# Attention and Mish MLP on one core: stores issued by ScalarE, loads a pair further ahead, an earlier DMA turn of q and k

## The chip, the cores and the metric

The kernel runs on one core of a Trainium2 chip. A core has five engines that work beside each other: TensorE (PE in the profile; PEld is its weight load), VectorE (DVE), ScalarE (ACT), GpSimd (POOL) and SyncE (SP), which issues most DMAs. Each engine takes its instructions in order. The metric is the device time of one execution in microseconds (us); a lower time is better. Three runs of the kernel before gave 464.16, 464.88 and 459.46 us, a median of 464.16.

## The reference

Inputs are q, k and v of 8 batches x 12 heads x 448 positions x 64, and the weights w_in (768 x 2048) and w_out (2048 x 768), all in float32. What is computed:

```python
scores = q @ k.T / sqrt(64)                   # per batch and head, 448 x 448
m = max(scores, axis=-1)
e = exp(scores - m)
attn = e / (sum(e) + exp(-m) + 1e-9)          # softmax with one more term in the sum
x = (attn @ v), heads side by side            # 3584 tokens x 768
h = x @ w_in                                  # 3584 x 2048
g = h * tanh(log(1 + exp(h)))                 # Mish
out = g @ w_out                               # 3584 x 768, float32
```

## The kernel before, in words

**Units.** Two heads side by side make a pair (128 partitions of q and k); six pairs make a batch, 48 pairs the whole. Three pairs are a unit (`UNIT_PAIRS`), so a batch has two units, and units 0 to 15 hold the attention; two more run out the MLP at the end. The loop variable is `u`, the unit's first pair is `p0`, and `nxt = p0 + 3` is the first pair of the next unit. Units u = 6 to 15 are the "joined" ones (`JOINED_FROM` is 6). The change concerns these.

**One joined unit** has two stretches.

- The *exponential stretch* follows the list `JOINED` (line 625), an order written out by hand. Its entries: `("s", n)` issues the products q k^T of step n (four steps per pair, twelve in all) on TensorE; `mA`, `mB`, `m` take row maxima on VectorE; `eA`, `eB`, `e` are the exponentials on ScalarE; `("fill", n)` puts n chunks of the second matmul (g @ w_out, line 543) of an older batch on TensorE; `("copy", i)` copies a finished w_out group from PSUM to the SBUF tile `o_sb` on VectorE (line 522) and, when a tile of 128 rows is complete, stores it (line 507); `("av", i)` is attn @ v of pair i of the unit before, `("avc", i)` its copy to xT; `("load", i)` loads a pair and casts one; `("turn", i)` turns q and k of a pair by DMA.
- The *Mish stretch* (from line 841) computes eight tiles of x @ w_in (line 442), each followed by Mish on ScalarE (line 481). Beside them VectorE and GpSimd normalise the unit's e, and SP issues the DMA transposes of e into eT (line 390), one per pair. Here the next unit's q and k are turned too: most pairs by TensorE (line 224) in front of the tiles f = 2, 4 and 6, with copies by VectorE and ScalarE; the pairs in `TURN_BY_DMA` (from pair 21 on the first of each unit, and pair 46) by a DMA transpose (line 237).

**Loads and casts.** `load_pair(p)` is three DMAs of 224 KB (q, k, v in float32), issued by SP, with four buffers per tensor. `cast_pair(p)` is three casts to bf16 on GpSimd (lines 201 to 207 and 188). q_bf and k_bf of the pair are what TensorE or the DMA turns; v_bf is wanted a unit later. In a joined unit the three `load` entries load the pairs p0 + 3, 4 and 5, which are the next unit's; the second and the third entry cast the pair loaded by the entry before, and the last pair, `nxt + 2`, is cast in the Mish stretch (line 875).

**Queues.** All loads, e's transposes, q's and k's DMA turns and the stores are issued by SP, in the order in which the program has them; a DMA that waits for its data holds up all behind it. Only the last tile's smaller parts are stored by ScalarE. A tile of 128 rows takes two store DMAs, as rows of one DMA share a segment of 112. Two such tiles are complete in most joined units, one in u = 6, 10 and 14.

**PSUM.** Eight banks of 128 x 512 float32. In the Mish stretch tile f goes into the banks `JOINED_MISH_BANK = (7, 0, 4, 2, 6, 1, 7, 6)`; bank 2 and bank 3 hold the scores of step 9, banks 0 and 1 those of step 8, banks 4 and 5 those of step 10.

Of the kernel before, what the change touches and what calls it, by code (L numbers as in the profile page):

```python
# [15 lines left out]
UNIT_PAIRS = 3  # L16
# [3 lines left out]
def kernel(  # L20
# [9 lines left out]
    nc = tc.nc  # L30
# [203 lines left out]
    def turn_by_dma(p):  # L234

        qk = qk_all[:, p % UNIT_PAIRS]
        nc.sync.dma_start_transpose(
            out=qk.rearrange("c s (t q) -> c (s t) q", q=SP_),
            in_=qk_bf[:, p % N_CAST].rearrange("q s t h d -> q (s t h d)"),
        )  # L240
        qkT[p] = qk[:, 0, :], qk[:, 1, :]
# [250 lines left out]
            out=mids[g][:, :, 64 * half : 64 * half + 64], in_=gT[b][:, :, at : at + 64]  # L492
        )

    def store_rows(g, i, o_sb, cols):

        parts, r = [], i * 128
        while r < (i + 1) * 128:
            n = min((i + 1) * 128, (r // SP_ + 1) * SP_) - r
            parts.append((r, n))  # L500
            r += n
        queues = [nc.sync, nc.scalar if (g, i) == (B // 2 - 1, 6) else nc.sync]
        for queue, (r, n) in zip(queues, sorted(parts, key=lambda part: -part[1])):
            seg = r // SP_
            b, t, c0 = 2 * g + seg // NT, seg % NT, r % SP_
            rows = out[b * S : (b + 1) * S, :].rearrange("(c t) m -> t c m", t=NT)
            queue.dma_start(
                out=rows[t, c0 : c0 + n, cols], in_=o_sb[r - i * 128 : r - i * 128 + n, cols]
            )
# [3 lines left out]
    def mm2_group(pieces, bank=None):  # L513

        st = {"at": 0, "o": bank, "evacs": []}

        def evac(g, i, q0, nq, at, last):
            cols, n_cols = slice(q0 * NQ, (q0 + nq) * NQ), nq * NQ
            if (g, i) not in o_sbs:
                o_sbs[g, i] = [o_pool.tile([128, d_model], FP32, tag="o_sb", name="o_sb"), 0]  # L520
            o_sb, have = o_sbs[g, i]
            nc.vector.tensor_copy(out=o_sb[:, cols], in_=st["o"][:, at : at + n_cols])  # L522
            if last and bank is None:
                mo_free.append(st["o"])
            o_sbs[g, i][1] = have + nq
            if (g, i) == (B // 2 - 1, 6):
                store_rows(g, i, o_sb, cols)
            elif have + nq == 24:
                store_rows(g, i, o_sb, slice(0, d_model))

        def chunk(k, f0, f1):
            g, i, q0, nq = pieces[k]
            if st["o"] is None:
                flush_late()
                st["o"] = mo_take()
            if i < 3:
                src, c0 = gT[2 * g], i * 128
            elif i == 3:
                src, c0 = mids[g], 0
            else:  # L540
                src, c0 = gT[2 * g + 1], i * 128 - S
            for ff in range(f0, f1):
                nc.tensor.matmul(  # L543
                    st["o"][:, st["at"] : st["at"] + nq * NQ],
                    lhsT=src[:, ff, c0 : c0 + 128],
                    rhs=w_out_sb[:, ff, q0 * NQ : (q0 + nq) * NQ],
                    start=(ff == 0), stop=(ff == FF_T - 1),
                )
            if f1 == FF_T:
                last = k == len(pieces) - 1  # L550
                args = (g, i, q0, nq, st["at"], last)
                st["evacs"].append(lambda: evac(*args))
                st["at"] += nq * NQ
                if last and bank is None:
                    late.extend(st["evacs"])

        step = 2
        chunks = [
            (lambda k=k, f0=f0: chunk(k, f0, f0 + step), pieces[k][3] / 6)
            for k in range(len(pieces))  # L560
            for f0 in range(0, FF_T, step)
        ]
        return chunks, st["evacs"]
# [8 lines left out]
    for g in range(B // 2):  # L572
# [50 lines left out]
        [],  # L623
    )
    JOINED = (
        ("mA", 1), ("fill", 2), ("mA", 0), ("fill", 1), ("mB", 0), ("fill", 1), ("eA", 1),
        ("load", 0), ("mB", 1), ("fill", 2), ("eA", 0), ("mB", 2), ("fill", 1), ("eB", 1),
        ("mA", 2), ("fill", 2), ("eB", 0), ("fill", 1), ("copy", 0), ("fill", 3), ("eB", 2),
# [4 lines left out]
        ("fill", 1), ("mB", 6), ("fill", 1), ("eA", 4), ("fill", 1), ("copy", 1), ("s", 11),  # L633
        ("eB", 6), ("load", 2), ("fill", 1), ("m", 11), ("fill", 1), ("eB", 5), ("fill", 1),
# [4 lines left out]
    )  # L639
    PART_BANK = (7, 6, 2)  # L640
    AV_BANK = (7, 3, 6)
# [79 lines left out]
    for u in range(UNITS_PER_B, N_UNITS + 2 * UNITS_PER_B):  # L721
# [16 lines left out]
        for what, arg in JOINED if joined else ():  # L738
            at, idx = p0 + arg, p0 * STEPS + arg
            heads = {"A": (0,), "B": (1,)}.get(what[-1], (0, 1))  # L740
            if what == "s":
                held[arg] = score_products(idx)
            elif what[0] == "m":
                score_maxima(*held[arg], heads)
            elif what[0] == "e":
                exps(idx, heads)
            elif what == "fill":
                for _ in range(arg):
                    filler.popleft()[0]()
            elif what == "copy":  # L750
                for evac in copies[arg]:
                    evac()
            elif what == "av":
                held["av", arg] = av_pair(at - UNIT_PAIRS, bank=joined_banks[AV_BANK[arg]])
            elif what == "avc":
                held["av", arg]()
            elif what == "load":
                load_pair(at + LEAD - 1)
                if arg:
                    cast_pair(at + LEAD - 2)  # L760
            elif nxt + arg in TURN_BY_DMA:
                turn_by_dma(nxt + arg)
        if joined:
            expm_of(nxt - 1)

# [75 lines left out]
        for f in range(FF_U):  # L841
# [28 lines left out]
            if f in (1, 3, 5):  # L870
                if nxt + f // 2 not in TURN_BY_DMA:
                    transpose_pair(nxt + f // 2, bank=f // 2 % 2)
                    evac_qk(nxt + f // 2)
                if f == 1 and u >= first_mm2:
                    cast_pair(nxt + UNIT_PAIRS - 1)
            if not to_group and f in (4, 6):
                scores_ahead(nxt * STEPS + f // 2 - 1)
# [48 lines left out]
```

## Time and profile before

| What | Value |
|---|---|
| median of three runs | 464.16 us (459.46 to 464.88) |
| the profiled execution, its own time | 462.32 us |
| its span, first to last instruction | 460.5 us |
| mean granted TensorE clock | 0.989 |
| PE busy | 427.1 us (93%) |
| DVE, ACT busy | 340.7 and 342.3 us (74% each) |
| POOL busy | 185.7 us (40%) |
| DMA, mean over the span | 201 GB/s, 92.66 MB |
| stores by SP, by ScalarE | 57 and 3 |
| DMA transposes of e, of q and k | 43 and 10 |

The page's times come from one execution. "Busy" counts work only, not issuing a DMA: SP's DMA issues have durations of their own, in rows with SPq (ACTq for ScalarE's). In a row such as "PE b L224 <- POOL qk_bf L201" the left side waits, and the right side is what ended the wait; L224 is line 224 of the kernel. A wait in square brackets in a row of the order of time is the engine's idle time just before that row. Matmuls overlap in the rows: six products of 448 columns follow each other in 1.14 us, though one of them is shown with 0.35 us.

### The profile page before, as it was taken

The numbers are of one execution on the slowest core, as the hardware profiler recorded it, in microseconds if no ns is written. First come the engines' busy times: TensorE is split into PE (matmuls) and PEld (weight loads), VectorE is DVE, ScalarE is ACT, GpSimd is POOL, SyncE is SP. The second block draws the span as 40 slices with busy tenths as digits, with TensorE's granted clock in tenths as the row PEclk, the third lists the DMA queues.
The fourth block names the chain that finished last, engine by engine and source line by source line (L and its number), as shares of the span: only waits on it lengthen the run. The fifth ranks groups of instructions, "written<-read, shape, count | busy, mean of one in ns | idle before, by whom it ended". The sixth has DMA issues, their size and how long they took to land.

```text
span 460.5 us, 8732 instructions
## 1 busy us (share of the span) xinstructions
PE 427.1 (93%) x2968; PEld 234.4 (51%) x2968; DVE 340.7 (74%) x756; ACT 342.3 (74%) x908; POOL 185.7 (40%) x352
## 2 busy tenths in 40 slices
PE   4586798899999999899999999999999999999996
PEld 2243445444445555455555545564555455555565
DVE  4899968878797888668788888888888888421021
ACT  5998988988797788688888887897979878211300
POOL 3666839253517161534436271715454360000000
PEclk9997999999999999999999999999999999999999
DMA  8999999997999989998999999999999995950213
GB/s 210 220 202 221 282 188 248 200 212 174 223 263 217 246 171 227 266 207 234 185 270 211 219 227 206 247 219 254 229 265 201 244 206 135 177 133 0 70 36 103
DMA packets 211661, 92.66 MB, mean 201 GB/s; under 512 B 168352, under 2 KB 208160, under 8 KB 211616
## 3 DMA queue, kind: packets, MB, share of 16 engines
q1 hardware_dynamic: 204032, 85.76, 87.4%
q0 software_dynamic: 7488, 6.29, 9.3%
q8 instruction: 23, 0.38, 0.3%
q14 instruction: 22, 0.18, 0.1%
q10 hardware_dynamic: 96, 0.05, 0.0%
HBM read 45.61 MB, written 11.01 MB: 123 GB/s over the span
## 4 chain that ended last, share of the span: by engine, by line
PE 65%; DMA 10%; DVE 9%; ACT 6%; issue 3%; SPq 3%; POOL 2%; POOLq 0%; DVEq 0%
PE mo L543 24%; PE mo L442 17%; DMA q_f<-in_q_dram 7%; PE b L442 7%; DVE negm L335 6%; PE b L543 5%; ACT en L347 5%; PE b L304 4%; PE mo L423 2%; DMA k_f<-in_k_dram 2%; PE b L224 2%; PE b L423 2%; DMA eT<-en 1%; PE mo L312 1%; DVE xT L432 1%
## 5 line engine op out<-in xcount | busy, mean ns | idle before, releaser
L347 ACT ACTIVATE en<-b,negm 128x448 bf16<-128x448 f32 x216 | 133.9, 636 | 20.9 <-DVE negm L335 20.9
L335 DVE TENSOR_REDUCE negm<-b 128x1 f32<-128x448 f32 x216 | 120.6, 614 | 21.2 <-PE b L307 21.2
L543 PE MATMUL mo<-w_out_sb,gT 128*128 128x384 bf16 (+3 forms) x736 | 107.5, 298 | 2.4 <-DVE o_sb L522 1.8
L543 PEld LDWEIGHTS <-gT 128*128 128x128 bf16 x896 | 82.4, 98 | 51.8 <-issue 10.5
L442 PEld LDWEIGHTS <-w_in_sb 128*128 128x128 bf16 x768 | 72.6, 98 | 67.7 <-issue 7.3
L442 PE MATMUL mo<-xT,w_in_sb 128*128 128x448 bf16 x480 | 102.7, 357 | 0.8 <-DVE xT L432 0.3
L481 ACT ACTIVATE gT<-mo 128x448 bf16<-128x448 f32 x73 | 40.2, 551 | 54.1 <-PE mo L442 53.7
L384 POOL TENSOR_SCALAR en<-en,rden 128x448 bf16<-128x448 bf16 x109 | 67.3, 634 | 23.5 <-DVE rden L378 15.5
L386 DVE TENSOR_SCALAR en<-en,rden 128x448 bf16<-128x448 bf16 x227 | 71.5, 384 | 0.7
L442 PE MATMUL b<-xT,w_in_sb 128*128 128x448 bf16 x282 | 58.8, 353 | 0.2 <-DVE xT L432 0.2
L347 ACT ACTIVATE en<-sc,negm 128x448 bf16<-128x448 f32 x84 | 52.5, 642 | 4.0 <-DVE negm L335 2.6
L522 DVE COPY o_sb<-mo 128x384 f32<-128x384 f32 (+3 forms) x54 | 25.8, 492 | 40.0 <-PE mo L543 39.4
L335 DVE TENSOR_REDUCE negm<-sc 128x2 f32<-128x896 f32 (+1 forms) x48 | 45.2, 966 | 6.0 <-PE sc L307 4.0
L203 POOL TENSOR_SCALAR qk_bf<-q_f 112x512 bf16<-112x512 f32 x18 | 11.1, 615 | 90.5 <-DMA q_f<-in_q_dram 90.5
L347 ACT ACTIVATION_READ_ACCUMULATOR en<-b,negm 128x1 f32 x216 | 45.1, 209 | 0.0
L188 POOL CAST v_bf<-v_f 112x512 bf16<-112x512 f32 x48 | 29.7, 619 | 14.1 <-DMA v_f<-in_v_dram 13.3
L201 POOL CAST qk_bf<-q_f 112x512 bf16<-112x512 f32 x29 | 19.2, 662 | 37.2 <-DMA q_f<-in_q_dram 36.9
L207 POOL CAST qk_bf<-k_f 112x512 bf16<-112x512 f32 x47 | 29.1, 618 | 6.0 <-DMA k_f<-in_k_dram 5.4
L224 PEld LDWEIGHTS <-qk_bf 112*128 112x128 bf16 x304 | 19.8, 104 | 22.2 <-DVE qk_bf L201 4.4
L423 PEld LDWEIGHTS <-v_bf 112*64 112x64 bf16 x384 | 20.1, 110 | 19.5 <-issue 9.2
L543 PE MATMUL b<-w_out_sb,gT 128*128 128x384 bf16 x160 | 29.3, 326 | 0.0
L304 PE MATMUL b<-qk_all 64*128 64x448 bf16 x108 | 29.0, 355 | 0.0
(71 smaller groups left out, 523.7 us busy)
## 6 DMA issues: line engine op xcount, KB each, us to landing
q_f<-in_q_dram SPq DMA_DIRECT2D x48, 224.0 KB, 5.3
k_f<-in_k_dram SPq DMA_DIRECT2D x48, 224.0 KB, 5.4
v_f<-in_v_dram SPq DMA_DIRECT2D x48, 224.0 KB, 5.6
w_in_sb<-in_moe_w_in_dram POOLq DMA_DIRECT2D x12, 256.0 KB, 6.1
w_out_sb<-in_moe_w_out_dram POOLq DMA_DIRECT2D x8, 384.0 KB, 7.7
out_dram<-o_sb SPq DMA_DIRECT2D x7, 336.0 KB, 5.1
out_dram<-o_sb SPq DMA_DIRECT2D x8, 288.0 KB, 4.8
out_dram<-o_sb SPq DMA_DIRECT2D x8, 240.0 KB, 5.4
```

Of the source, the lines that this page charges most:

```text
L188: nc.gpsimd.tensor_copy(out=casted[p][2], in_=loaded.pop(p)[2])
L207: cast_k(out=k_bf, in_=k_f.rearrange(by_t, t=NT))
L224: nc.tensor.transpose(by_s[s][:, t * SP_ : (t + 1) * SP_], src[:, t].rearrange("p h d -> p (h d)"), ident[:SP_, :SP_],)
L304: nc.tensor.matmul(sc[0][:, 0:S], lhsT=qT[0:64, qa : qa + 128], rhs=kA, start=True, stop=True)
L335: nc.vector.tensor_reduce(out=negm, in_=scored, axis=AX.X, op=ALU.max, negate=True)
L347: nc.scalar.activation(out=st["en"][:, :, c, 0:SP_], in_=sc[bk][:, 0:S].rearrange("q (j c) -> q j c", j=NT), func=AF.Exp, bias=st["negm"][ ...
L384: nc.gpsimd.tensor_scalar(scalar2=1.0, op0=ALU.mult, op1=ALU.mult, **args)
L386: nc.vector.tensor_scalar(scalar2=None, op0=ALU.mult, **args)
L423: nc.tensor.matmul(av[h * 64 : (h + 1) * 64, 0:S], lhsT=v_bf[:, h, j * D : (j + 1) * D], rhs=e_h, start=(j == 0), stop=(j == NT - 1),)
L442: nc.tensor.matmul(h_ps[:, 0:S], lhsT=w_in_sb[:, dm, ff * 128 : (ff + 1) * 128], rhs=xT[b][:, dm, :], start=(dm == 0), stop=(dm == DM_T - 1),)
L481: nc.scalar.activation(out=gT[b][:, ff, :], in_=h_ps[:, 0:S], func=AF.Mish)
L543: nc.tensor.matmul(st["o"][:, st["at"] : st["at"] + nq * NQ], lhsT=src[:, ff, c0 : c0 + 128], rhs=w_out_sb[:, ff, q0 * NQ : (q0 + nq) * NQ ...
```

## The change

Three things are altered, all in the joined units:

- **Stores.** A complete tile is not stored at its copy, but put on a list (`to_store`); the entry `("store", 0)`, behind the last copy of attn @ v and in front of the exponentials of step 9, issues what is on the list from ScalarE. Outside the joined units SP issues the stores as before.
- **Loads.** From u = 7 on the three load entries load p0 + 4, 5 and 6; u = 6 loads one pair more at its end. The casts move with them: the new entry `("cast", 0)` near the head of the unit casts `nxt`, the second load entry `nxt + 1`, the third `nxt + 2`, and the cast in the Mish stretch is gone.
- **The DMA turn.** `("turn", 0)` moves from behind the exponentials of step 8 to behind `("s", 3)`, ahead of the unit's loads. As the entry for the first load is moved behind it, SP has the turn directly behind the transposes of e. In u = 6 the turn stays at the unit's end.

```diff
--- before.py
+++ after.py
@@ -492,14 +492,16 @@
             out=mids[g][:, :, 64 * half : 64 * half + 64], in_=gT[b][:, :, at : at + 64]
         )
 
-    def store_rows(g, i, o_sb, cols):
+    to_store = []
+
+    def store_rows(g, i, o_sb, cols, queue=nc.sync):
 
         parts, r = [], i * 128
         while r < (i + 1) * 128:
             n = min((i + 1) * 128, (r // SP_ + 1) * SP_) - r
             parts.append((r, n))
             r += n
-        queues = [nc.sync, nc.scalar if (g, i) == (B // 2 - 1, 6) else nc.sync]
+        queues = [queue, nc.scalar if (g, i) == (B // 2 - 1, 6) else queue]
         for queue, (r, n) in zip(queues, sorted(parts, key=lambda part: -part[1])):
             seg = r // SP_
             b, t, c0 = 2 * g + seg // NT, seg % NT, r % SP_
@@ -526,7 +528,10 @@
             if (g, i) == (B // 2 - 1, 6):
                 store_rows(g, i, o_sb, cols)
             elif have + nq == 24:
-                store_rows(g, i, o_sb, slice(0, d_model))
+                if bank is None:
+                    store_rows(g, i, o_sb, slice(0, d_model))
+                else:
+                    to_store.append((g, i, o_sb, slice(0, d_model), nc.scalar))
 
         def chunk(k, f0, f1):
             g, i, q0, nq = pieces[k]
@@ -623,19 +628,19 @@
         [],
     )
     JOINED = (
-        ("mA", 1), ("fill", 2), ("mA", 0), ("fill", 1), ("mB", 0), ("fill", 1), ("eA", 1),
-        ("load", 0), ("mB", 1), ("fill", 2), ("eA", 0), ("mB", 2), ("fill", 1), ("eB", 1),
+        ("mA", 1), ("cast", 0), ("fill", 2), ("mA", 0), ("fill", 1), ("mB", 0), ("fill", 1),
+        ("eA", 1), ("mB", 1), ("fill", 2), ("eA", 0), ("mB", 2), ("fill", 1), ("eB", 1),
         ("mA", 2), ("fill", 2), ("eB", 0), ("fill", 1), ("copy", 0), ("fill", 3), ("eB", 2),
-        ("fill", 3), ("s", 3), ("eA", 2), ("fill", 1), ("m", 3), ("s", 5), ("s", 4), ("s", 6),
-        ("mA", 5), ("e", 3), ("fill", 1), ("mA", 6), ("fill", 1), ("eA", 5), ("load", 1),
-        ("fill", 1), ("mB", 5), ("fill", 1), ("eA", 6), ("fill", 1), ("mB", 4), ("s", 7),
-        ("fill", 2), ("m", 7), ("eB", 4), ("fill", 1), ("mA", 4), ("fill", 1), ("e", 7),
-        ("fill", 1), ("mB", 6), ("fill", 1), ("eA", 4), ("fill", 1), ("copy", 1), ("s", 11),
-        ("eB", 6), ("load", 2), ("fill", 1), ("m", 11), ("fill", 1), ("eB", 5), ("fill", 1),
-        ("s", 10), ("e", 11), ("copy", 2), ("s", 8), ("av", 1), ("mA", 10), ("mA", 8),
-        ("eA", 10), ("av", 0), ("avc", 1), ("eA", 8), ("turn", 0), ("av", 2), ("avc", 0),
-        ("mB", 8), ("s", 9), ("mB", 9), ("avc", 2), ("eB", 9), ("mA", 9), ("eB", 8), ("mB", 10),
-        ("eA", 9), ("eB", 10), ("turn", 1),
+        ("fill", 3), ("s", 3), ("turn", 0), ("load", 0), ("eA", 2), ("fill", 1), ("m", 3),
+        ("s", 5), ("s", 4), ("s", 6), ("mA", 5), ("e", 3), ("fill", 1), ("mA", 6), ("fill", 1),
+        ("eA", 5), ("load", 1), ("fill", 1), ("mB", 5), ("fill", 1), ("eA", 6), ("fill", 1),
+        ("mB", 4), ("s", 7), ("fill", 2), ("m", 7), ("eB", 4), ("fill", 1), ("mA", 4),
+        ("fill", 1), ("e", 7), ("fill", 1), ("mB", 6), ("fill", 1), ("eA", 4), ("fill", 1),
+        ("copy", 1), ("s", 11), ("eB", 6), ("load", 2), ("fill", 1), ("m", 11), ("fill", 1),
+        ("eB", 5), ("fill", 1), ("s", 10), ("e", 11), ("copy", 2), ("s", 8), ("av", 1),
+        ("mA", 10), ("mA", 8), ("eA", 10), ("av", 0), ("avc", 1), ("eA", 8), ("av", 2),
+        ("avc", 0), ("mB", 8), ("s", 9), ("mB", 9), ("avc", 2), ("store", 0), ("eB", 9),
+        ("mA", 9), ("eB", 8), ("mB", 10), ("eA", 9), ("eB", 10), ("turn", 1),
     )
     PART_BANK = (7, 6, 2)
     AV_BANK = (7, 3, 6)
@@ -747,6 +752,9 @@
             elif what == "fill":
                 for _ in range(arg):
                     filler.popleft()[0]()
+            elif what == "store":
+                while to_store:
+                    store_rows(*to_store.pop(0))
             elif what == "copy":
                 for evac in copies[arg]:
                     evac()
@@ -754,12 +762,20 @@
                 held["av", arg] = av_pair(at - UNIT_PAIRS, bank=joined_banks[AV_BANK[arg]])
             elif what == "avc":
                 held["av", arg]()
+            elif what == "cast":
+                if u > JOINED_FROM:
+                    cast_pair(nxt)
             elif what == "load":
-                load_pair(at + LEAD - 1)
+                lead = LEAD - 1 if u == JOINED_FROM else LEAD
+                load_pair(at + lead)
                 if arg:
-                    cast_pair(at + LEAD - 2)
-            elif nxt + arg in TURN_BY_DMA:
-                turn_by_dma(nxt + arg)
+                    cast_pair(at + lead - 1)
+            elif u > JOINED_FROM:
+                if nxt + arg in TURN_BY_DMA:
+                    turn_by_dma(nxt + arg)
+            elif arg:
+                turn_by_dma(nxt)
+                load_pair(nxt + UNIT_PAIRS)
         if joined:
             expm_of(nxt - 1)
 
@@ -871,7 +887,7 @@
                 if nxt + f // 2 not in TURN_BY_DMA:
                     transpose_pair(nxt + f // 2, bank=f // 2 % 2)
                     evac_qk(nxt + f // 2)
-                if f == 1 and u >= first_mm2:
+                if f == 1 and first_mm2 <= u <= JOINED_FROM:
                     cast_pair(nxt + UNIT_PAIRS - 1)
             if not to_group and f in (4, 6):
                 scores_ahead(nxt * STEPS + f // 2 - 1)
```

## The prediction

> **What bounds the kernel now.** I read the page's busy shares first, then a view that cuts the time into the ten joined units (u = 6 to 15, each from its first product with w_out to the next one's), then TensorE's waits, and last the order of time on the queues around the longest wait.
>
> ```profile
> span 460.5 us, 8732 instructions
> ...
> 145.92:170.33 24.41, 24.41 (x174) 13.54 (x175) 21.07 (x49) 20.91 (x57) 10.06 (x21) 1.00 1.03 203
> 170.33:198.50 28.17, 26.38 (x174) 13.86 (x175) 20.62 (x48) 21.09 (x57) 14.01 (x27) 0.94 1.09 237
> 198.50:222.90 24.40, 24.40 (x174) 13.49 (x175) 20.21 (x49) 20.83 (x57) 9.73 (x20) 1.00 0.97 207
> 222.90:247.65 24.75, 24.58 (x174) 13.53 (x175) 20.84 (x48) 21.02 (x57) 10.51 (x22) 1.00 1.11 245
> 247.65:273.28 25.63, 24.75 (x174) 13.57 (x175) 21.79 (x49) 21.21 (x57) 11.58 (x24) 1.00 1.05 220
> 273.28:297.68 24.40, 24.40 (x174) 13.54 (x175) 20.84 (x48) 20.91 (x57) 10.91 (x22) 1.00 1.10 233
> 297.68:322.43 24.75, 24.57 (x174) 13.53 (x175) 21.15 (x49) 21.02 (x57) 10.26 (x22) 1.00 1.13 226
> 322.43:346.90 24.47, 24.47 (x174) 13.61 (x175) 20.61 (x48) 20.93 (x57) 12.63 (x25) 1.00 1.08 245
> 346.90:372.41 25.51, 24.34 (x166) 13.08 (x167) 21.96 (x48) 20.58 (x56) 10.91 (x22) 1.00 1.18 222
> 372.41:395.98 23.57, 22.94 (x154) 12.57 (x153) 20.48 (x51) 19.98 (x54) 3.65 (x8) 1.00 0.76 155
> ```
>
> A row is a stretch in us, its length, then busy time and instructions of PE, PEld, DVE, ACT and POOL, then the granted clock, the share of the DMA engines and GB/s. In u = 6, 8 and 11 PE is busy for the whole 24.40 us: with nothing late a unit costs TensorE's own 24.40 us, and no other engine comes near (DVE 21, ACT 21). What lies above that is 3.77 us in u = 7, 0.35 in u = 9, 1.23 in u = 10, 0.35 in u = 12, 0.07 in u = 13 and 1.11 in u = 14, in all 6.88 us. TensorE's waits from 120 us on say what it is:
>
> ```profile
> PE b L224 <- POOL qk_bf L201: 2.5, 2, 1.6
> PE b L224 <- POOL qk_bf L207: 1.6, 5, 0.8
> PE b L423 <- DMA eT<-en: 0.9, 1, 0.9
> ```
>
> The columns are us in total, times, longest. The transposes of q and k on TensorE wait for GpSimd's casts, 4.1 us in seven waits. The worst one, in u = 7, in order of time on SP, POOL and PE, with the clock just behind it:
>
> ```profile
> 182.98 3.43 SPq L507 DMA_DIRECT2D out_dram<-o_sb  x4
> 186.45 0.59 SPq L158 DMA_DIRECT2D q_f<-in_q_dram  x1
> 191.59 1.34 POOL L201 CAST qk_bf<-q_f 112x512 bf16<-112x512 f32 x1 [2.76 <-DMA q_f<-in_q_dram]
> 192.99 0.37 PE L224 MATMUL b<-ident,qk_bf 112*128 112x112 bf16 x4 [1.61 <-POOL qk_bf L201]
> 194.47:197.88 3.41, 3.41 (x12) 1.19 (x11) 0.00 (x0) 0.71 (x3) 3.21 (x8) 0.50 1.05 223
> ```
>
> SP issues in order. The four stores wait there for VectorE's copies and hold the unit's third load back until 186.45; its q lands 5 us later, the cast follows, and TensorE stands for 1.61 us. For 3.41 us after that the clock is 0.50, which costs 1.71 us more. 1.61 + 0.19 (the k half) + 1.71 is 3.5 of the 3.77 us of u = 7.
>
> **The change part by part.** *Loads a pair ahead, casts out of the Mish stretch.* The same loads, casts and bytes; each slot of a unit now serves the next pair. An ordinary unit on SP, and the casts that end its third and second slot:
>
> ```profile
> 218.34 13.59 SPq L390 DMA_TRANSPOSE eT<-en  x3
> 231.99 0.57 SPq L158 DMA_DIRECT2D q_f<-in_q_dram  x1
> 235.16 0.87 SPq L507 DMA_DIRECT2D out_dram<-o_sb  x2
> 236.08 0.44 SPq L158 DMA_DIRECT2D q_f<-in_q_dram  x1
> 239.81 2.12 SPq L237 DMA_TRANSPOSE qk_all<-qk_bf  x1
> 235.25 0.62 POOL L203 TENSOR_SCALAR qk_bf<-q_f 112x512 bf16<-112x512 f32 x1 [9.40 <-DMA q_f<-in_q_dram]
> 239.14 0.61 POOL L207 CAST qk_bf<-k_f 112x512 bf16<-112x512 f32 x1
> 243.62 0.65 POOL L207 CAST qk_bf<-k_f 112x512 bf16<-112x512 f32 x1
> 244.33 0.37 PE L224 MATMUL b<-ident,qk_bf 112*128 112x112 bf16 x4 [0.17 <-POOL qk_bf L207]
> 222.74 1.69 DVE L335 TENSOR_REDUCE negm<-b 128x1 f32<-128x448 f32 x3 [1.64 <-PE b L307]
> ```
>
> The pair that TensorE turns last is cast from the third slot, done at 244.27, and wanted at 244.16: late by 0.1 to 0.2. After the change it comes from the second slot, done here at 239.75, so 4.4 us earlier. Against that stands what is put ahead of the loads, next. The new cast at the head of a unit has its data from the unit before, and GpSimd stands idle there for 9.40 us up to 235.25. VectorE loses GpSimd's casts as company during its normalising; the 1.64 us that it then waits for TensorE (222.74) cover what it gains, so I count nothing.
>
> *The DMA turn right behind e's.* Moved from the end of SP's list to ahead of the nine loads. Its issue takes this long:
>
> ```profile
> L237 SPq DMA_TRANSPOSE qk_all<-qk_bf x10: 1222/1319/2116, 160.8 to 366.2; - x10
> ```
>
> (min, median, max in ns.) So every load is issued 1.3 us later, at most 2.1. The second slot loses 1.3 and gives back nothing else: 4.4 - 1.3 leaves 3 us of the 4.4, less what the turn's bytes take of the DMA engines, which the trace doesn't show by itself; between 0 (the queue has gaps) and the turn's 5 us to landing. I take 1 us, since SP's issue and not the DMA engines spaces these loads; 2 us remain. The turn waits for that new cast, three operations of 0.6 us in GpSimd's idle time from 225.9 on, and for s 3, ahead of it in the list; SP leaves e's transposes at 231.9, so it doesn't wait. What is late next is the pair that TensorE turns before that; it moves from the second slot to the first, so its wait of 0.8 us in u = 10 goes too. The last wait for a POOL cast is then gone and TensorE meets its own 24.40 us.
>
> *The stores on ScalarE.* In the ten joined units 34 stores (two in u = 6, 10 and 14, four in the other seven) leave SP and stand on ScalarE behind the exponentials of group 8. What ScalarE does at that place, in every unit alike, and TensorE's products that need its banks:
>
> ```profile
> 237.42 0.63 ACT L347 ACTIVATE en<-b,negm 128x448 bf16<-128x448 f32 x1 [1.45 <-DVE negm L335]
> 238.66 0.63 ACT L347 ACTIVATE en<-b,negm 128x448 bf16<-128x448 f32 x1
> 237.72 3.57 PE L442 MATMUL b<-xT,w_in_sb 128*128 128x448 bf16 x18
> ```
>
> There is a hole of 1.45 us, as VectorE still looks for the maxima of group 9. Behind the store stand four exponentials. The third of them (238.66, done at 239.29) frees bank 2, into which the Mish stretch's fourth tile goes: the products 13 to 18 of that row, so from 237.72 + 12 x 0.189 = 239.99 on (0.189 us a product: 3.57 less the last one's 0.35, over 17). That is a slack of 0.70 us. Stores may take 1.45 + 0.70 = 2.15 us in all, 0.54 each of four, before TensorE waits; e's transposes start later by the same lateness; TensorE waited for eT only once (0.9 us, above), so there is slack of a size not shown, and I count nothing for half a microsecond.
>
> What a store costs ScalarE under load, no row shows. The nearest:
>
> ```profile
> L507 SPq DMA_DIRECT2D out_dram<-o_sb x57: 316/424/1673, 129.9 to 457.4; - x57
> q10 hardware_dynamic: 96, 0.05, 0.0%
> L507 ACTq DMA_DIRECT2D out_dram<-o_sb x3: 376/377/395, 453.7 to 457.4; - x3
> 456.10 0.32 SPq L507 DMA_DIRECT2D out_dram<-o_sb  x1
> 456.11 0.38 ACTq L507 DMA_DIRECT2D out_dram<-o_sb  x1
> 205.60 1.33 SPq L158 DMA_DIRECT2D v_f<-in_v_dram  x1
> ```
>
> Below: 0.38 each, 1.52 for four, all but 0.07 us in the hole. Above: SP's longest, 1.67, so 6.7 for four, 5.2 late, 4.5 us of TensorE in each of seven units. I take 0.50 (ScalarE's 0.38 against SP's 0.32 beside it, scaled to SP's median of 0.42 in the loop): four take 2.0, 0.55 late, inside the 0.70. Two fit in the hole. So the stores cost nothing, with little to spare.
>
> On the price of an issue there is a rule that speaks against the change. The Trainium skill (Perfetto Trace Analysis, DMA Instruction — HWDGE) says that the two issuing sequencers share one descriptor generator, locked for one instruction at a time, and that the reported duration holds the wait for the lock. By it ScalarE's stores, at the hour of SP's loads, would each wait for one of them; the issue pair at 456.10 and 456.11, where 0.32 and 0.38 run side by side, speaks against a full wait. It is a rival below.
>
> **The sum.** The profiled execution took 462.32 us, 460.5 of it span. Less 6.9 is 455.4; I leave 1 us for cast waits that remain in a unit with slow loads and for a store now and then over its 0.54: 456.5. The three runs shown have a median of 464.16, 1.84 above the profiled one; that difference of runs would be of the same stalls, so I stay with the profiled basis. 456.5 is 1.7% under the median. About 2% is what a measurement of this kernel can tell from no change.
>
> **The rivals.** *Stores wait for SP's loads* (one generator): 0.38 + 0.46 (a load's issue on SP, 0.44 to 0.57 in the rows above) = 0.84 each, four 3.36, 1.91 late, 1.21 us of TensorE in seven units, 8.5 in all: 455.4 + 8.5 = 463.9, no gain. For it: the loads are issued in those very microseconds. Against: the pair at 456.10.
>
> *Slower than before: stores under back-pressure.* About 13 us into a unit SP has put e's transposes, the turn and several loads into the queues, and it is there that its own issues stretch to 1.33 us (205.60). If ScalarE's do, four take 5.3, 3.9 late, 3.2 us of TensorE in seven units, and two take 2.7, 0.5 us in three: 455.4 + 22.4 + 1.5 = 479. The point that decides: 6.9 us over seven units is 1.0 us late beyond the 0.70, so 3.15 us for four, 0.79 each; under it there is a gain, over it a loss. Against: ScalarE's issues have a queue of their own (q10; SP's is another), and SP's stores at 235.16 took 0.87 for two at that hour.
>
> *Loads are late all the same.* The turn's bytes delay the loads by all of its 5 us in the units that now stall: about half of 6.9 stays, 459.
>
> *Nothing of it reaches the end*: the store's move and the earlier loads only shift the wait to e's transposes (0.9 us for eT is in the waits above): 462 to 464.
>
> *The clock stays low.* The Trainium skill (TensorE: Matmul & The Clock Gate, HAM oscillation) warns of idle gaps beyond about 3.4 us; here 1.80 us in two pieces stood before the half clock, so by that rule the stall is not its cause. What it would do here: the 0.50 stretch comes back somewhere, 1.7 us, and the time is 457.1 + 1 = 458.2. The row at 194.47, right behind the longest wait and the only such stretch in the joined units, makes me doubt it.
>
> **How the numbers follow.** Chances: the forecast 0.55; stores wait for loads 0.12; back-pressure 0.07; loads late 0.12; nothing reaches the end 0.06; the clock stays low 0.08. The range runs from 453.5 (all of the 6.9 gone and two more, as in the shortest of the runs shown, 459.46 against 462.32) to 466, which holds all rivals but the back-pressure. Faster by over 2% is under 454.9: the forecast with nothing left over, 0.2. Slower by over 2% is over 473.4, 1.19 us a store: the back-pressure and a little beside, 0.09. The rest, 0.71, lies within.
>
> **What the profile after would show.** No wait of PE L224 for POOL from u = 7 on, units of 24.4 us and a clock of 1.00 in all of them; POOL's last cast of a unit before 242 in a unit like that at 222.9; four ACTq issues of about 0.5 us in a hole before group 9's exponentials, and those no more than 0.6 us later. Wrong it would be if these issues took over 0.8 us, if PE waited for ACT's en at the fourth Mish tile, or if a load issued behind the turn landed after 8 us.

## The result: slower, 485.6 us against a forecast of 456.5

The changed kernel took 485.56 us (median of four runs, 483.71 to 489.98); the kernel before, beside it, 461.81 us (four runs, 458.14 to 464.88). The ratio is 1.053 with a 95% interval of 1.041 to 1.065. The forecast was a gain of 1.7% with a range of 453.5 to 466.0.

The profile after, first the joined units, cut as before from one unit's first product with w_out to the next one's (here u = 6 to 10 and 15). The columns are the stretch, its length, busy time and instructions of PE, PEld, DVE, ACT and POOL, the granted clock, the DMA engines' share and GB/s.

```profile
147.09:173.64 26.55, 24.54 (x175) 13.52 (x174) 19.99 (x49) 20.84 (x57) 10.49 (x22) 1.00 1.05 220
173.64:204.50 30.86, 27.44 (x176) 14.54 (x174) 19.79 (x48) 21.13 (x57) 14.26 (x29) 0.89 0.93 209
204.50:230.13 25.63, 24.55 (x175) 13.53 (x174) 20.01 (x49) 20.86 (x57) 7.95 (x17) 1.00 0.97 202
230.13:260.44 30.31, 26.14 (x175) 14.19 (x174) 19.77 (x48) 21.12 (x57) 13.01 (x26) 0.94 0.95 207
260.44:284.85 24.41, 24.41 (x175) 13.53 (x174) 20.40 (x49) 20.87 (x57) 8.81 (x19) 1.00 0.91 208
...
393.45:417.08 23.63, 23.00 (x154) 12.63 (x153) 20.55 (x51) 20.03 (x54) 4.03 (x8) 1.00 0.80 168
```

The ten units take 270.0 us (147.09 to 417.08) where they took 250.1. All units with four stores beside loads (u = 7 to 9 and 11 to 13) are long, and so is u = 6 with two; u = 10 and u = 14 with two are at TensorE's own time (24.41 and 24.00), and u = 15, which has four stores and no loads, stands still for 0.6 us only. TensorE's waits in these units (us in total, times, longest):

```profile
PE b L442 <- ACT en L347: 20.1, 7, 4.2
PE mo L548 <- ACT gT L481: 0.6, 1, 0.6
```

The casts are gone as a wait, as forecast. In their place are 20.1 us in seven waits for ScalarE's exponentials, five times as much. The timeline of u = 7 (start, length, engine, line, operation; in brackets the idle time before it and what the profile takes for its end), first ScalarE:

```profile
186.07 0.62 ACT L347 ACTIVATE en<-b,negm 128x448 bf16<-128x448 f32 x1
186.58 0.20 ACT L347 ACTIVATION_READ_ACCUMULATOR en<-b,negm 128x1 f32 x1
189.59 2.75 ACTq L509 DMA_DIRECT2D out_dram<-o_sb  x4
192.38 0.63 ACT L347 ACTIVATE en<-b,negm 128x448 bf16<-128x448 f32 x1 [5.60 <-DMA k_f<-in_k_dram]
```

SP at the same time:

```profile
183.93 0.57 SPq L158 DMA_DIRECT2D q_f<-in_q_dram  x1
...
189.09 0.46 SPq L158 DMA_DIRECT2D v_f<-in_v_dram  x1
```

And TensorE:

```profile
194.39 2.40 PE L442 MATMUL b<-xT,w_in_sb 128*128 128x448 bf16 x6 [3.42 <-ACT en L347]
```

SP issues its nine loads from 183.93 to 189.55. ScalarE is free at 186.78 (186.58 + 0.20). Its stores are issued at 189.59, 190.39, 191.14 and 191.86 and take until 192.34. The hole of 1.45 us has become 5.60. That is 4.15 us late; less the slack of 0.70 it makes 3.45, and TensorE waits 3.42. The idle times before that exponential in u = 6, 8, 9, 11, 12 and 13 (4.18, 3.25, 6.35, 6.38, 4.01 and 5.55 us), less 2.15, give 2.0, 1.1, 4.2, 4.2, 1.9 and 3.4; TensorE's waits are 2.0, 1.1, 4.2, 4.2, 1.8 and 3.4.

What the stores wait for is in the trace. For every DMA it names the semaphore that the landing raises (its completion semaphore) and the one that the issue waits for. All DMAs of SP and ScalarE in the joined units take turns on eight such semaphores, in the order of the program, so a DMA is issued only when the one that had its semaphore before, eight places ahead, has landed. The four stores of u = 7 wait in this way for k_f issued at 184.56, v_f at 185.07, q_f at 185.57 and k_f at 186.07. These land 5.0, 5.3, 5.6 and 5.8 us after their issue (189.57, 190.37, 191.12, 191.84), and each store begins 0.02 us behind. The wait in brackets above names the last of them, and GpSimd's casts of the first two begin at the same moments:

```profile
189.62 0.61 POOL L207 CAST qk_bf<-k_f 112x512 bf16<-112x512 f32 x1 [1.57 <-DMA k_f<-in_k_dram]
190.49 0.61 POOL L188 CAST v_bf<-v_f 112x512 bf16<-112x512 f32 x1 [0.26 <-DMA v_f<-in_v_dram]
```

Of the 34 stores in the joined units 29 begin 0.02 us behind such a landing; the others are the first one of u = 8 and the four of u = 15. That SP's last load of u = 7 is issued by 189.55, just ahead of the first store, is a coincidence: SP is silent while the other three stores wait.

In three units the clock is halved from late in the wait on (columns as in the first fence):

```profile
193.50:200.30 6.80, 5.91 (x22) 2.76 (x22) 4.48 (x18) 5.61 (x14) 1.43 (x5) 0.50 0.44 118
251.50:254.90 3.40, 3.27 (x15) 1.73 (x15) 2.49 (x10) 3.37 (x8) 0.00 (x0) 0.50 0.34 134
306.10:309.50 3.40, 3.13 (x15) 1.76 (x15) 2.35 (x10) 3.37 (x9) 0.00 (x0) 0.50 0.43 165
```

At half speed 13.6 us cost 6.8 where TensorE has work, which it has from the end of the wait on. The waits and the half clock, 26.9 at most, stand against 4.1 of cast waits and 1.7 of half clock before: 21.1 more, of which the ten units, 19.9 longer, show nearly all.

### The profile page after: what moved, and what is told of

The parts are those of the page before. It is cut to its first block, busy times and chain, and to the rows that moved or that the text cites. A ratio compares the mean times of both kernels' runs of the same rounds, so it can differ in the third digit from the quotient of the medians.

```text
span 481.5 us, 8708 instructions
## 1 busy us (share of the span) xinstructions
PE 432.3 (90%) x2968; PEld 236.3 (49%) x2968; DVE 332.1 (69%) x756; ACT 342.3 (71%) x908; POOL 184.2 (38%) x352
## 4 chain that ended last, share of the span: by engine, by line
PE 49%; DMA 13%; SPq 11%; DVE 10%; ACT 8%; POOL 5%; issue 3%; ACTq 1%; POOLq 0%; DVEq 0%
PE mo L548 16%; PE mo L442 14%; DMA k_f<-in_k_dram 9%; PE b L442 7%; ACT en L347 7%; DVE negm L335 6%; SPq L390 6%; SPq L158 4%; POOL en L384 3%; PE b L304 2%; DMA q_f<-in_q_dram 2%; PE b L224 2%; PE b L548 2%; PE mo L423 2%; SPq L237 2%
## 5 line engine op out<-in xcount | busy, mean ns | idle before, releaser
L548 PEld LDWEIGHTS <-gT 128*128 128x128 bf16 x896 | 82.4, 98 | 51.8 <-issue 10.4
L442 PE MATMUL b<-xT,w_in_sb 128*128 128x448 bf16 x282 | 63.5, 368 | 20.2 <-ACT en L347 20.1
L386 DVE TENSOR_SCALAR en<-en,rden 128x448 bf16<-128x448 bf16 x227 | 63.9, 351 | 0.7
L201 POOL CAST qk_bf<-q_f 112x512 bf16<-112x512 f32 x29 | 17.9, 618 | 89.6 <-DMA q_f<-in_q_dram 89.2
L363 DVE SCALAR_TENSOR_TENSOR den<-sums,expm 128x21 f32<-128x21 f32 (+1 forms) x20 | 4.1, 203 | 40.3 <-ACT expm L360 40.3
```

Source lines behind the costliest of these rows:

```text
L386: nc.vector.tensor_scalar(scalar2=None, op0=ALU.mult, **args)
L442: nc.tensor.matmul(h_ps[:, 0:S], lhsT=w_in_sb[:, dm, ff * 128 : (ff + 1) * 128], rhs=xT[b][:, dm, :], start=(dm == 0), stop=(dm == DM_T - 1),)
L548: nc.tensor.matmul(st["o"][:, st["at"] : st["at"] + nq * NQ], lhsT=src[:, ff, c0 : c0 + 128], rhs=w_out_sb[:, ff, q0 * NQ : (q0 + nq) * NQ ...
```

## The experiments

Each run shares a chip with runs of the kernel before (medians of 464.2 to 465.8 us there). A time without a ratio is that of a single execution. L numbers in the fences are those of the kernel named, and waits are those of TensorE in the joined units, unless said otherwise.

### One part alone, one part undone

**Only the stores.** The kernel before, with the store list and its entry, and nothing else of the change:

```diff
+                    to_store.append((g, i, o_sb, slice(0, d_model), nc.scalar))
-        ("mB", 8), ("s", 9), ("mB", 9), ("avc", 2), ("eB", 9), ...
+        ("mB", 8), ("s", 9), ("mB", 9), ("avc", 2), ("store", 0), ("eB", 9), ...
```

> The kernel before with this one part of the change: complete tiles are listed and ScalarE stores them behind the last copy of attn @ v. Theory: SP is in its loads and the turn at that hour in the old order too, so ScalarE stands for about 3 us in each unit with four stores: 470 to 482 us. Rival (it takes the new order, with all nine loads in one burst behind the turn): within 2 us of the kernel before, 458 to 464 us.

Measured: 483.76 us, ratio 1.0415 (1.0335 to 1.0496). The same wait, in the profile of this run:

```profile
PE b L442 <- ACT en L347: 19.3, 8, 3.5
```

The stores on ScalarE alone make the loss; it takes neither the new order of the loads nor the early turn. My expectation was a little low, and it named SP's issuing where 28 of the 34 stores begin 0.02 us behind the landing of a load, as in the changed kernel.

**Only the stores undone.** Two forms: SP issues the listed stores at the new place, or SP stores at the copies as before.

```diff
-                    to_store.append((g, i, o_sb, slice(0, d_model), nc.scalar))
+                    to_store.append((g, i, o_sb, slice(0, d_model), nc.sync))
```

> The changed kernel, but SP issues the listed stores at the same place of the order. Theory (ScalarE's stores wait behind SP's burst of loads): TensorE's 20.1 us of waits for ScalarE's exponentials go, and with them the two or three half-clock stretches; 454 to 459 us, the time that was forecast. Rival (the loads a pair ahead or the turn in front of them are what costs): the time stays above 470 us.

```diff
-                if bank is None:
-                    store_rows(g, i, o_sb, slice(0, d_model))
-                else:
-                    to_store.append((g, i, o_sb, slice(0, d_model), nc.scalar))
+                store_rows(g, i, o_sb, slice(0, d_model))
```

> The changed kernel with all stores back on SP at their copies, as in the kernel before: the loads, the casts and the turn are all that is left of the change. Theory: 454 to 458 us, faster than before by 4 to 8 us, no wait of TensorE for a cast. Rival (the earlier loads only move the wait to e's transposes or the stores hold the loads back again): 459 to 463 us, as before.

Measured: 462.57 us, ratio 0.9973 (0.9935 to 1.0011), and 461.47 us, ratio 0.9948 (0.9906 to 0.9990). The wait for ScalarE is gone in both, so what costs is settled. In the first form SP has the wait in ScalarE's place (SP's waits in the joined units; L509 is the store):

```profile
SPq L509 <- DMA v_f<-in_v_dram: 4.0, 8, 1.4
SPq L509 <- DMA q_f<-in_q_dram: 3.9, 6, 0.8
SPq L509 <- DMA k_f<-in_k_dram: 2.5, 6, 0.6
```

The same stores at the same place stand 10.4 us for landings of loads, but on an engine that computes nothing. The time that was forecast doesn't come all the same: the gain is 0.3% (an interval that holds no change) and 0.5%, where 1.7% was forecast. TensorE's largest wait in the second form:

```profile
PE mo L423 <- DMA eT<-en: 2.4, 3, 1.1
```

Three of its units, u = 8 to 10:

```profile
198.21:222.82 24.61, 24.59 (x176) 13.61 (x174) 21.26 (x49) 20.94 (x57) 11.08 (x23) 1.00 1.10 228
222.82:247.86 25.04, 24.59 (x176) 13.61 (x174) 20.93 (x48) 20.93 (x57) 11.44 (x24) 1.00 1.06 237
247.86:273.55 25.69, 24.59 (x175) 13.61 (x174) 21.51 (x49) 20.93 (x57) 10.55 (x23) 1.00 1.05 220
```

The wait for casts has been changed for waits for e's transposes (2.4 us, and one of 1.1 at another tile), where the kernel before had a single one of 0.9 in its whole run. It is the rival of e's transposes that takes most of the gain.

### What makes e's transposes late

The same kernel (stores on SP at the copies), but q and k of the pairs from 25 on are loaded in 16 of 256 columns; the casts of these pairs take those alone, and the rest of their q and k is stale.

```diff
+            part = 16 if p > 24 and nm != "v" else NT * D
-                out=t, in_=src[b, h0 : h0 + 2].rearrange(...)
+                out=t[:, :, 0:part], in_=src[b, h0 : h0 + 2].rearrange(...)[:, :, 0:part]
```

> As the run with all stores on SP at their copies, with the same small loads of q and k (output not the reference's). Theory (with the casts out of the way the DMA queues bind the steady units: e's transposes queue behind loads and stores): with a quarter of the bytes gone the units u = 8 to 13 take TensorE's own 24.4 us each, where the run with full loads had 24.4 to 25.7, and no wait for eT is left there. Rival (e's transposes are late because SP's list of issues is long): the waits for eT stay.

Measured: 455.66 us in a single run. The units u = 7 to 9, to which those up to u = 13 are alike:

```profile
170.35:194.74 24.39, 24.39 (x175) 13.53 (x173) 20.04 (x48) 20.90 (x57) 10.59 (x25) 1.00 0.96 198
194.74:219.14 24.40, 24.40 (x175) 13.54 (x173) 20.16 (x49) 20.91 (x57) 8.48 (x23) 1.00 0.99 181
219.14:243.54 24.40, 24.40 (x175) 13.54 (x173) 19.69 (x48) 20.91 (x57) 9.03 (x23) 1.00 0.95 200
```

Every steady unit takes TensorE's 24.40 us, and the time is near the one that I had forecast for the change. SP issues as many DMAs as before, so its list isn't too long by the number of issues. But it waits in it: with full loads SP's issues in u = 7 to 13 wait 7.5 us in all for the landings of earlier loads, by the same semaphores as ScalarE's stores, and here for none. The first transpose of e is issued 20.8 to 22.4 us into these units with full loads, and 19.7 to 20.1 us here. So the bytes count (a DMA share of 0.95 to 0.99 in the units shown instead of 1.05 to 1.10), and at least in part because SP's list waits for them to land. The casts take less of GpSimd here too, which this run does not separate; but no wait for a cast was left to shorten.

### What a store costs ScalarE, and why

**ScalarE busy without any DMA.** Stores on SP at the copies, and eight copies of 128x448 that nothing needs at the place of ScalarE's stores:

```diff
             elif what == "store":
-                while to_store:
-                    store_rows(*to_store.pop(0))
+                for _ in range(8):
+                    nc.scalar.copy(idle, w_in_sb[:, 0, 0:S])
```

> All stores on SP at their copies, and in the place of ScalarE's stores eight copies of 128x448 on ScalarE that nothing needs, some 0.45 us each (the spacing of its copies and Mish tiles in the Mish stretch): 3.6 us without a DMA. Theory (ScalarE late at this place is what costs, whatever makes it late; the hole is 1.45 us and the slack behind it 0.70): 1.45 us of TensorE's wait for ScalarE's exponentials in each of ten units, 14 us in all, 474 to 480 us. Rival (the slack is larger, and the stores cost by what they do to the DMA queues): under 5 us of such waits, 461 to 466 us.

Measured: 488.98 us in a single run. ScalarE in one unit:

```profile
189.86 0.20 ACT L348 ACTIVATION_READ_ACCUMULATOR en<-b,negm 128x1 f32 x1
189.95 4.73 ACT L755 COPY idle<-w_in_sb 128x448 bf16<-128x448 bf16 x8
194.59 0.63 ACT L348 ACTIVATE en<-b,negm 128x448 bf16<-128x448 f32 x1
```

TensorE's wait in the ten units:

```profile
PE b L443 <- ACT en L348: 23.6, 10, 2.4
```

The eight copies took 4.73 us, about 0.58 each and not 0.45, so the expected total was too low; but the arithmetic of the slack is exact. From the end of ScalarE's work (189.86 + 0.20 = 190.06) to 194.59 are 4.53 us; less 1.45 and 0.70 that leaves 2.38, and TensorE waits 2.36 in the mean of ten units. Lateness of ScalarE at this place is enough for the whole effect; nothing special about a DMA is needed.

**The stores where SP is silent.** The entry moves behind the unit's last exponential:

```diff
-        ("avc", 0), ("mB", 8), ("s", 9), ("mB", 9), ("avc", 2), ("store", 0), ("eB", 9), ...
+        ("avc", 0), ("mB", 8), ("s", 9), ("mB", 9), ("avc", 2), ("eB", 9), ...
-        ... ("eB", 10), ("turn", 1),
+        ... ("eB", 10), ("store", 0), ("turn", 1),
```

> The changed kernel with the ScalarE stores moved behind the last exponential of the unit, some 4 us later, when SP has issued its loads and issues nothing. Theory: no wait for SP any more; four stores take 1.5 us if nothing else holds them, 3.6 us if the 0.9 us from one to the next in the changed kernel comes from full queues; 456 to 466 us. Rival (a store costs ScalarE 0.9 us wherever it stands): 3.6 us late at the Mish stretch in seven units, 2 us over its slack: 468 us or more.

Measured: 475.11 us, ratio 1.0225 (1.0141 to 1.0309), above what the theory allowed. SP in one unit, its last load and what it issues next:

```profile
243.99 0.46 SPq L158 DMA_DIRECT2D v_f<-in_v_dram  x1
252.21 4.21 SPq L390 DMA_TRANSPOSE eT<-en  x1
```

ScalarE there:

```profile
245.01 0.33 ACTq L509 DMA_DIRECT2D out_dram<-o_sb  x1
245.68 0.35 ACTq L509 DMA_DIRECT2D out_dram<-o_sb  x1
246.63 2.87 ACTq L509 DMA_DIRECT2D out_dram<-o_sb  x2
249.54 0.22 ACT L360 ACTIVATE expm<-negm 128x21 f32<-128x21 f32 x1 [3.55 <-DMA k_f<-in_k_dram]
```

SP issues nothing from 244.45 to 252.21, and yet only the first store goes out at once. The other three (245.68, 246.63 and 249.17) begin 0.02 us behind the landings of v_f issued at 240.99, q_f at 241.49 and k_f at 241.99, whose semaphores they have; the last of these takes 7.2 us to land. So it isn't SP's issuing that the stores wait for. ScalarE's lateness then meets the Mish tiles: TensorE waits 9.1 us for Mish in six waits, and behind the joined units 4.4 us for eT.

**The stores where SP issues e's transposes.** The entry moves to the next unit's head, behind the exponentials of step 2 (u = 15's own are flushed at its end):

```diff
-        ("fill", 3), ("s", 3), ("turn", 0), ...
+        ("store", 0), ("fill", 3), ("s", 3), ("turn", 0), ...
```

> The changed kernel with ScalarE's stores moved to the next unit's head, behind the exponentials of step 2, where SP issues e's transposes one after the other at 4.3 us each. Theory A (one issue at a time, SP first): ScalarE stands until SP's transposes are all issued, about 6 us in each unit, and the time goes over 510 us. Theory B (no exclusion, only full queues): four stores take 1.5 to 4 us, 462 to 485 us.

Measured: 534.95 us in a single run. One unit, ScalarE:

```profile
238.44 0.33 ACTq L509 DMA_DIRECT2D out_dram<-o_sb  x1
238.81 1.22 ACTq L509 DMA_DIRECT2D out_dram<-o_sb  x1
240.07 9.91 ACTq L509 DMA_DIRECT2D out_dram<-o_sb  x2
250.03 0.63 ACT L347 ACTIVATE en<-b,negm 128x448 bf16<-128x448 f32 x1 [9.83 <-DMA eT<-en]
```

SP there:

```profile
230.97 16.67 SPq L390 DMA_TRANSPOSE eT<-en  x3
```

The time is over the 510 us of theory A, but not for its reason. Three stores are issued while SP issues transposes; the DMAs that had their semaphores before had landed at least 17 us earlier. The fourth, issued at 249.60, has the semaphore of SP's third transpose and begins 0.02 us after that one landed. The same holds for all six waits of TensorE for ScalarE in this run, 61.2 us in all. Beside this the two queues do lengthen each other's issues: ScalarE's second and third store take 1.22 and 1.61 us to issue, and SP's three transposes 16.67, where those of the kernel before in the same place, shown in the prediction, took 13.59. What makes them longer no run separates.

**ScalarE's stores beside small loads.** The changed kernel with q and k loaded in 16 columns, as above.

> The changed kernel, ScalarE storing, but from pair 25 on each load of q and k moves 16 of its 256 columns (as many issues, 252 KB a pair instead of 672 KB), and their casts take those alone; q and k of these pairs are stale, so the output is not the reference's. Theory A (ScalarE's issue stands behind SP's burst of nine issues, whatever they carry): the first store of a unit still comes only when SP's last load is issued, and TensorE's waits for ScalarE stay at 12 us or more in all. Theory B (the queues are full of bytes): stores are issued at once and 0.4 to 0.5 us apart, TensorE's waits for ScalarE under 4 us, 458 to 464 us.

Measured: 476.98 us in a single run, and 11.4 us of waits for ScalarE in five waits. ScalarE in the worst unit:

```profile
241.82 5.93 ACTq L516 DMA_DIRECT2D out_dram<-o_sb  x4
247.80 0.63 ACT L354 ACTIVATE en<-b,negm 128x448 bf16<-128x448 f32 x1 [6.28 <-DMA k_f<-in_k_dram]
```

Neither theory holds as put. In most units the first store now gets out between two of SP's loads, near the beginning of the hole, against theory A; later ones still wait, against theory B. In this unit the second begins 0.02 us behind the landing of v_f issued at 240.39, which is loaded whole, and the fourth (247.43) behind that of the small k_f issued at 241.40; the third store and SP's own last load take 2.46 and 2.54 us to issue in between. Smaller loads halve the wait, they don't end it.

**Stores beside no loads** are in the changed kernel itself: u = 15 has four stores and no loads, and SP is silent. ScalarE there:

```profile
405.79 0.32 ACTq L509 DMA_DIRECT2D out_dram<-o_sb  x1
406.15 0.44 ACTq L509 DMA_DIRECT2D out_dram<-o_sb  x1
406.63 1.14 ACTq L509 DMA_DIRECT2D out_dram<-o_sb  x2
408.04 0.63 ACT L347 ACTIVATE en<-b,negm 128x448 bf16<-128x448 f32 x1 [1.45 <-DVE negm L335]
```

Four stores in 1.98 us (405.79 to 407.77), 0.50 each, two of them issued beside ScalarE's last activation, all before the hole ends, and the exponential is released by VectorE as before. The DMAs that had their semaphores before had landed at least 16 us earlier. The price of 0.50 was right for this case alone.

### The other queue, and the turn's place

**The turn late.** Stores on SP at their copies, loads a pair ahead, the turn at its old place behind the exponentials of step 8.

```diff
-        ("fill", 3), ("s", 3), ("turn", 0), ("load", 0), ...
+        ("fill", 3), ("s", 3), ("load", 0), ...
-        ... ("eA", 8), ("av", 2),
+        ... ("eA", 8), ("turn", 0), ("av", 2),
```

> Loads a pair ahead and no cast in the Mish stretch, stores on SP at their copies, but the DMA turn stays where it was, behind the exponentials of step 8, after the loads. Theory (the turn's place matters little; the same DMAs in all): within 2 us of the run with the early turn, 459 to 463 us. Rival (the early turn delays loads and stores so that e's transposes start late): 455 to 459 us.

Measured: 460.39 us, ratio 0.9925 (0.9892 to 0.9959). Of the waits for eT one of 1.1 us is left, behind the joined units, and two for the turn have come:

```profile
PE b L304 <- DMA qk_all<-qk_bf: 1.7, 2, 1.2
```

**The turn between the second and the third load**, stores on SP at their copies:

```diff
-        ("eA", 5), ("load", 1), ("fill", 1), ...
+        ("eA", 5), ("load", 1), ("turn", 0), ("fill", 1), ...
```

> Loads a pair ahead, all stores on SP at their copies, the turn between the second and the third load of the unit. Theory (only the third load can wait, and the turn is wanted by the unit's end): neither the waits for qk_all of the late turn nor the waits for eT of the early one: 456 to 460 us. Rival (the queues are full, so any order moves the wait elsewhere): 460 to 462 us, as both.

Measured: 458.83 us, ratio 0.9876 (0.9792 to 0.9960), the fastest kernel that does all of the work, 1.2% below the kernel before and 5.5% below the changed one. Waits for eT are left in its joined units:

```profile
PE mo L423 <- DMA eT<-en: 2.5, 2, 1.9
```

Its interval overlaps those of the late and of the early turn, so which place is best is not settled.

**GpSimd issues the listed stores**, with the late turn and with the turn between the loads (`nc.gpsimd` in the place of `nc.scalar`, else as the two kernels above).

> Loads a pair ahead, the turn at its old place, the listed stores issued by GpSimd at the unit's end. Theory (SP's list and the full queues are what is left to gain from; GpSimd is idle): the stores' 2 us leave SP and the turn is issued that much earlier, so the two waits for qk_all (1.7 us) go: 457 to 460 us. Rival (GpSimd's own issue is slow or stands in front of its normalising): 462 us or more.

> The same with the turn between the second and the third load, and GpSimd issuing the listed stores. Theory: the best of these, 455 to 459 us. Rival: as the late turn with GpSimd's stores.

Measured: 480.77 us, ratio 1.0322 (1.0227 to 1.0417), and 475.09 us, ratio 1.0199 (1.0115 to 1.0283). Both were expected to gain. In the second, GpSimd's four stores in one unit:

```profile
190.33 2.16 POOL L509 DMA_DIRECT2D out_dram<-o_sb  x4
```

SP's issues of e's transposes beside them:

```profile
190.57 19.22 SPq L390 DMA_TRANSPOSE eT<-en  x3
```

TensorE's largest wait, in the whole run:

```profile
PE mo L423 <- DMA eT<-en: 11.5, 6, 3.2
```

The three transposes take 6.75, 7.97 and 4.28 us, 19.2 with the gaps between them, against 13.59; TensorE then waits for eT. GpSimd's own issues, about 0.55 us each, are not the cost: its stores have other semaphores and wait for no landing (in this unit those were last used some 100 us before). They go out just as SP begins e's transposes. That this is the transposes' company and not the place of the entry was not tried with another place, and why they stretch so far stays open.

## Why the prediction was wrong, point by point

- **TensorE's own 24.40 us a unit, and casts as what stands above it: right.** With small loads seven units in a row take 24.40, and no wait for a cast is left in the joined units of the changed kernel.
- **The stores' place, the hole of 1.45 us and the slack of 0.70: right.** Eight idle copies and the seven waits of the changed kernel agree with it to a tenth of a microsecond.
- **The step that failed: "I take 0.50".** By this term of the sum four stores take 2.0 us and stay inside the slack. In the six units with four stores beside loads ScalarE stood idle 3.25 to 6.38 us, in u = 7 5.60 for four, 1.4 each. The issues themselves are as short as I took them (0.32 us; the changed kernel's median of 37 is 0.323). What I put at nothing is the wait ahead of them, for the landing of a load whose semaphore the store has. The price of 0.50 us holds only where that DMA has long landed, as in u = 15. I scaled a row of an issue; I should have asked how long the engine stands and what an issue waits for beside its data. SP's waits in the kernel before have the answer, stores that wait for loads they have no data from: `SPq L507 <- DMA q_f<-in_q_dram: 1.6, 3, 0.9`.
- **Two rivals were near it, neither with this mechanism.** "Stores wait for SP's loads" has each store wait for the issue of one load, 0.84 us a store and 463.9 us; they wait for landings, 3.1 to 6.1 us behind the issue. The stores under back-pressure, with 0.79 us as the point that decides and 479 us as the price, put the time into longer issues, which stayed short. That this price is the nearest to what came is luck.
- **The rule on the shared generator did not decide.** The pair at 456.10 and 456.11 is of the quiet tail and was thin evidence against it. The Trainium skill (Perfetto Trace Analysis, DMA Instruction — HWDGE) has the reported duration of a DMA instruction begin when its semaphores are satisfied, and the wait for the lock lie inside it. The trace agrees with the first: the stores' waits for landings stand ahead of rows of 0.32 us. A wait for the lock would lengthen the rows; ScalarE's longest in the changed kernel has 0.60 us, and beside SP's transposes there are 1.22 and 1.61, which no run puts down to the lock or to something else.
- **A reading of the kernel before was off.** The four stores at 182.98 don't wait for VectorE's copies: SP issues them one behind the other, and the first alone takes 1.67 us.
- **"The stores cost nothing" and "TensorE meets its own 24.40 us": the second failed too.** Without ScalarE's stores the gain is 0.3 to 0.5% and not 1.7%. My answer to what is late next was the other pair's cast; it is e's transposes, and with less to load (a share under 1) their waits are gone. I had read the share of 1.05 and more in the units' rows as nothing that binds.
- **The clock.** That the half clock follows a stall was right: every such stretch in the joined units of the changed kernel begins late in a wait of 3.4 to 4.2 us (u = 7, 9 and 11). But u = 13's 3.4 us brings none, and of the ten waits of 2.36 us beside the idle copies three do, so it is no fixed price. The granted clock of the changed kernel changes on a grid of 3.41 us (at 193.45, 200.28, 251.48, 254.89, 306.09 and 309.51), so where a wait falls on it may decide; no run tests that.

What stays open: no run gives ScalarE's stores completion semaphores of their own beside loads, so what they would cost without this wait is seen only where nothing is left to land (0.50 us each in u = 15) and beside the transposes. Why some loads take over 7 us to land, and why transposes and stores lengthen each other's issues, is open too.

## What to carry to other kernels

A DMA that is moved to a compute engine's queue is paid in that engine's time, and its price is the time that the engine stands idle around it, at that hour, and not the length of the issue's row. Before moving it, ask for which landing its issue has to wait. In this program eight completion semaphores are shared by all DMAs of SP and ScalarE, so a store behind a burst of nine loads stands until one of those loads has landed, here 3.1 to 6.1 us after its issue. On SP that wait costs only what stands behind it in SP's list; on ScalarE it costs exponentials. Put the price at which the slack is gone (here 0.54 us a store) beside that wait, not beside the median issue. And where SP's list waits for landings as well, removing the wait for one transfer gives back only what the next transfer has to spare.

## What the hardware showed that was not expected

- ScalarE stood 2.8 us ahead of one store (u = 7 of the changed kernel) and 7.9 us ahead of another (the stores beside e's transposes), with issues of 0.32 and 0.39 us behind it: a store is not issued before the DMA that had its completion semaphore has landed, and 29 of the 34 in the changed kernel's joined units begin 0.02 us after that.
- SP's own DMA transposes stretch in the units where another queue stores among them: three took 16.7 us beside ScalarE's stores and 19.2 beside GpSimd's, where 13.59 stood before.
- GpSimd as the issuer, with 0.55 us an issue, gave ratios of 1.032 and 1.020 to the kernel before, where the same turns with SP's stores at the copies gave 0.9925 and 0.9876.
